# A fused attention and gated feed-forward kernel: the second query block in two halves, and the order of jobs, fetches and roots around it

## The chip, the cores and the metric

The kernel runs on one core of a Trainium2 chip. The metric is the device time of one execution in microseconds, lower is better. Each kernel is judged by the median of several runs; one further execution is profiled.

## The reference

```python
def _layernorm(x, axis=-1, eps=1e-5):
    m = jnp.mean(x, axis=axis, keepdims=True)
    v = jnp.var(x, axis=axis, keepdims=True)
    return (x - m) / jnp.sqrt(v + eps)

def reference(A_x, A_wqkv, A_wo, B_x, B_w_gate, B_w_up, B_w_down):
    def _A_ref(x, wqkv, wo):                       # B=1, S=2048, D=640, H=32, Dh=20
        qkv = (x @ wqkv).reshape(B, S, 3, H, Dh).transpose(2, 0, 3, 1, 4)
        q, k, v = qkv[0], qkv[1], qkv[2]
        scores = jnp.einsum("bhqd,bhkd->bhqk", q, k) * (Dh ** -0.5)
        p = softmax(scores)
        o = jnp.einsum("bhqk,bhkd->bhqd", p, v)
        return o.transpose(0, 2, 1, 3).reshape(B, S, D) @ wo
    def _B_ref(x, w_gate, w_up, w_down):           # F=1728
        g = x @ w_gate
        u = x @ w_up
        return (g * u) @ w_down
    h = A_x + _A_ref(_layernorm(A_x), A_wqkv, A_wo)
    return h + _B_ref(_layernorm(h), B_w_gate, B_w_up, B_w_down)
```

All tensors are bf16.

## The kernel before

**Work and tiles.** The 2048 queries are four blocks of 512 (`QB`), the 32 heads eight groups of four (`HPG`), the 2048 keys sixteen tiles of 128. A head takes a slot of 32 partitions, so the four heads of a group are computed side by side in the TensorE array. Scores are made transposed, keys on partitions. A score tile (`sc`, L533) is 1536 columns, three PSUM banks; a bank is one head and key tile against 512 queries, or two key tiles against 256 queries. ScalarE takes the exponential of a score tile into an `E` tile (L547); 683 tiles hold all scores. There are two score tiles (`slot`) and six `E` buffers. TensorE then multiplies `E` with the values (`emit_AV`, L740; a value round is up to `AV_ROUNDS` units for each head), with a column of ones that gives the softmax sums, and VectorE drains the accumulator `acc` into `asb` (L752).

**Segments.** The tiles run through a list of segments `segs`, each a pass and a group of heads. A pass is a block or half of one: "0" to "3" are whole blocks, "C" and "D" are the halves of block 2, "A" and "B" those of block 3. `SPLIT_G` groups of a split block run whole and first; then the others run for the first half and after that for the second. Blocks 0 and 1 run whole; the first four groups of block 0 run by chunks of keys, as these are projected.

**Takes.** Where `x_takes` allows it, VectorE computes the exponential of the last bank of a tile, in four instructions (L580, L590, L591, L585) into `xe`; the ScalarE instruction is then 1024 columns instead of 1536. I call this a take. Among the conditions: the segment is not one of the chunked ones, the tile holds one segment alone, at least `X_LEAST` tiles of the segment follow, fewer than `X_OUT` taken banks wait for use, VectorE isn't behind, ScalarE isn't waiting for scores, and in the last block `room()`: 700 ns (`TILE_NS`) for each tile left must exceed the outstanding jobs (`PE_NS`, and `PART_NS` for each part still to open) by more than `ROOM`.

**The order.** The program is written out tile by tile by a planner that keeps model clocks (`at`): scores of tile i, value rounds, then jobs until shortly before the next scores must go (`run_job`). Jobs are Python generators in queues (`jobs`, `urgent`, `waiting`): first the projections of keys, values and queries, then the tails. If nothing is left to run, two padding matmuls keep TensorE busy (`keep_warm`, L496). `later(n, f)` runs f n tiles on. VectorE's spare time goes to takes under way and to small generators (`aux`). The order on each engine is fixed when the program is built.

**Norms and tails.** The softmax sums of a segment are inverted and spread by transfers over SP's queue (`norm`: L636, L637, L649, L652); for the segments in `FAST` by TensorE instead (`job_norm`). When all groups of a part are normed, `add_tail` opens its tail: output projection (`job_out`, L978), layer norm with the root on GpSimd (`rstd_steps`), transposes (L283), the gated layer (`job_glu`; whole blocks L1065, halves L1083), and the down projection (`job_y`, L1129). The up and gate weights are fetched for each of seven steps (L1036, buffers for two steps); in block 3 some are resident. The queries are written to DRAM (`spill`) for a general path that runs only if the softmax sums leave their range. Transfers are issued by SP in order.

**The end.** After the last tile, `last_tail` computes the tail of B with six PSUM banks: out projection (L1230, L1234), layer norm, and, while VectorE and ScalarE normalize, `fill` runs the jobs that are left; of A's down projection the last of four half rows is `held` back for this. Then transposes, gated layer (L1065) and down projection (L1129).

Of the kernel before, what the change touches and what calls it, by code (L numbers as in the profile page):

```python
# [19 lines left out]
P = 128  # L20
# [22 lines left out]
SPLIT_G = 2  # L43
# [17 lines left out]
RES_STEPS = 3  # L61
# [24 lines left out]
def kernel(  # L86
# [42 lines left out]
    huge = const.tile([P, 1], F32, name="huge")  # L129
    wo = [const.tile([P, D], BF16, name=f"wo{g}") for g in range(NG)]  # L130
# [52 lines left out]
    nc.gpsimd.memset(huge[:], 3.0e38)  # L183
    for c in range(KT):
        nc.vector.memset(wpad[c][:].rearrange("p m h e -> p (m h) e")[:, :, DH:SLOT], 0.0)
# [18 lines left out]
    def rstd_steps(mv, n, made, ve_=None):  # L204
# [11 lines left out]
        yield 1000 if ve_ is nc.vector else 50  # L216
        y = small.tile([P, n], F32, name="y")
        ve_.tensor_scalar(y[:].bitcast(I32), v[:].bitcast(I32), -0.5, float(0x5F3759DF), ALU.mult, ALU.add)
        t = small.tile([P, n], F32, name="nt")
        for k in range(3):  # L220
            ve_.tensor_tensor(t[:], y[:], y[:], ALU.mult)
            if ve_ is nc.gpsimd:
                ve_.tensor_tensor(t[:], t[:], v[:], ALU.mult)
                ve_.tensor_scalar(t[:], t[:], -0.5, 1.5, ALU.mult, ALU.add)
                ve_.tensor_tensor(y[:], t[:], y[:], ALU.mult)
            else:
                ve_.scalar_tensor_tensor(t[:], t[:], -0.5, v[:], ALU.mult, ALU.mult)
                ve_.scalar_tensor_tensor(y[:], t[:], 1.5, y[:], ALU.add, ALU.mult)
            if k != 2:
                yield (800, 600)[k] if ve_ is nc.vector else 50  # L230
        den = small.tile([P, n], BF16, name="den")
        ve_.tensor_tensor(den[:], v[:], y[:], ALU.mult)
# [81 lines left out]
    def job_V(t, half):  # L314
        ps = bank()
        for c in range(KT):
# [12 lines left out]
            "C": (2, 0, HW), "D": (2, HW, HW), "A": (3, 0, HW), "B": (3, HW, HW)}  # L329
# [621 lines left out]
    def load_wd():  # L951
        for f in range(2 * FP):
            p0 = max(0, (f + 1) * P - FF)
            if p0:
                nc.gpsimd.memset(late["Wd"][f][0:p0, :], 0.0)
# [488 lines left out]
```

## Time and profile before

| | us |
|---|---|
| median of 3 runs | 916.38 (915.68 to 917.12) |
| the profiled execution | 916.05 |
| its span, first to last instruction | 914.0 |
| ScalarE busy | 866.2 (95%) |
| TensorE matmuls busy | 817.5 (89%) |
| VectorE busy | 702.1 (77%) |
| GpSimd busy | 57.4 (6%) |

A row of grouped instructions reads: line, engine, operation, output<-input, shapes, count | busy us, mean ns of one | idle us of the engine just before them, and what ended it. A row of the timeline: start us, length us, engine, line, operation, count, and in brackets the idle time before it with what ended it. A row of the chain of waits: start, length, what. A row of windows: the stretch, its length, then busy us and count of each engine asked for, the clock granted to TensorE as a share of full speed, the busy share of the DMA engines, GB/s. Times run from the start of the span. The mean of a ScalarE instruction includes the part in which it overlaps with the next.

### The profile page before, as it was taken

The page shows a single profiled execution, that of the slowest core. Times are in us where ns is not written, and L with a number is a line of the kernel's source. Part 1 is how long each engine was busy: PE and PEld are TensorE (multiplying, and loading weights), DVE is VectorE, ACT ScalarE, POOL GpSimd, SP SyncE. Part 2 cuts the span into 40 slices and gives each one's busy share as a digit, 9 for nine tenths or more (in the row PEclk, how much of TensorE's full clock was granted, in tenths as well). Part 3 has the DMA queues.
Part 4 walks back from the last instruction along what each step waited for, and adds up shares of the span by engine and source line. Part 5 has one row for each costly group of instructions (what it writes and reads, how often), then busy time and mean ns, then how long its engine had stood idle before and what let it go on. Part 6 is the DMA issues. An engine that isn't in the chain of part 4 may idle for free.

```text
span 914.0 us, 20094 instructions
## 1 busy us (share of the span) xinstructions
PE 817.5 (89%) x8035; PEld 346.8 (38%) x8115; DVE 702.1 (77%) x1310; ACT 866.2 (95%) x719; POOL 57.4 (6%) x255
## 2 busy tenths in 40 slices
PE   8788999889989899899897888999998999998897
PEld 5233333222223222233232333434434445444575
DVE  8664349899999899899998999798998784542243
ACT  6999999999999999999999999999999999999931
POOL 4210000000001200000003000020001000010000
PEclk9999999999999999999999999999999999999999
DMA  6000011011025022212410022021411211201310
GB/s 195 17 14 1 1 27 27 14 24 37 4 61 149 13 71 72 64 49 90 160 28 14 20 70 68 19 54 49 117 51 42 73 28 51 57 15 50 80 44 18
DMA packets 74203, 46.54 MB, mean 51 GB/s; under 512 B 20380, under 2 KB 70440, under 8 KB 74104
## 3 DMA queue, kind: packets, MB, share of 16 engines
q1 hardware_dynamic: 74104, 45.20, 18.0%
q8 instruction: 65, 1.06, 0.5%
q14 instruction: 34, 0.28, 0.1%
HBM read 37.88 MB, written 7.30 MB: 49 GB/s over the span
## 4 chain that ended last, share of the span: by engine, by line
ACT 67%; issue 17%; PE 10%; DVE 4%; DMA 1%; POOL 1%; SPq 0%; ACTq 0%
ACT E L547 67%; PE sc L533 2%; PE f L1065 2%; PE f L1129 2%; PE acc L740 1%; DVE st L201 1%; PE mi L303 1%; PE mi L978 0%; PE f L1230 0%; PE mi L496 0%; DMA wu<-in_B_w_up_dram 0%; PE mi L317 0%; PE mi L1083 0%; DVE kT L310 0%; DVE vx L270 0%
## 5 line engine op out<-in xcount | busy, mean ns | idle before, releaser
L547 ACT ACTIVATE E<-sc 128x1536 bf16<-128x1536 f32 (+1 forms) x683 | 848.7, 1417 | 6.2 <-PE sc L533 5.9
L533 PE MATMUL sc<-qa,kT 32*128 32x512 bf16 (+1 forms) x1920 | 203.2, 340 | 28.6 <-ACT E L547 16.9
L533 PEld LDWEIGHTS <-kT 32*128 32x128 bf16 x2816 | 84.1, 91 | 244.6 <-issue 206.1
L740 PE MATMUL acc<-E,vx 128*32 128x256 bf16 (+1 forms) x2592 | 170.3, 326 | 1.7 <-DVE vx L270 1.2
L580 DVE TENSOR_SCALAR xv<-sc 128x512 f32<-128x512 f32 x167 | 115.0, 689 | 30.2 <-PE sc L533 26.5
L585 DVE SCALAR_TENSOR_TENSOR xe<-xt,xv 128x512 int16<-128x512 f32 x167 | 113.3, 682 | 1.0
L591 DVE SCALAR_TENSOR_TENSOR xt<-xt,xv 128x512 f32<-128x512 f32 x167 | 112.3, 681 | 0.5
L590 DVE SCALAR_TENSOR_TENSOR xt<-xv 128x512 f32<-128x512 uint16 x167 | 112.0, 683 | 0.3
L303 PE MATMUL mi<-lnT,wp 128*128 128x512 bf16 x279 | 83.3, 381 | 11.7 <-DVE qa L310 5.5
L740 PEld LDWEIGHTS <-vx 128*32 128x32 bf16 x2816 | 55.8, 95 | 66.4 <-issue 63.8
L533 PE MATMUL sc<-qb,kT 32*128 32x256 bf16 (+1 forms) x896 | 68.2, 288 | 8.1 <-ACT E L547 5.3
L1129 PE MATMUL mi<-wd,hh 128*128 128x320 bf16 x336 | 58.2, 301 | 1.6 <-DVE xr L1133 1.6
L740 PE MATMUL acc<-xe,vx 128*32 128x512 bf16 (+1 forms) x224 | 50.6, 332 | 0.0
L1129 PEld LDWEIGHTS <-hh 128*128 128x128 bf16 x448 | 38.7, 97 | 30.6 <-issue 18.7
L303 PEld LDWEIGHTS <-wp 128*128 128x128 bf16 x310 | 25.0, 97 | 55.9 <-issue 44.3
L310 DVE TENSOR_SCALAR kT<-mi,one_row 128x512 bf16<-128x512 f32 x30 | 22.5, 750 | 28.1 <-PE mi L303 24.7
L1065 PE MATMUL mi<-ln2T,wg 128*128 128x512 bf16 x128 | 38.0, 382 | 5.8 <-DVE u L270 5.2
L496 PE MATMUL mi<-kT,ident 128*128 128x512 bf16 x116 | 37.8, 386 | 5.5 <-DVE ln2T L270 1.0
L978 PE MATMUL mi<-wo,on 128*128 128x320 bf16 x224 | 40.5, 301 | 2.2 <-DVE xr L982 2.0
L1065 PE MATMUL mi<-ln2T,wu 128*128 128x512 bf16 x128 | 37.3, 382 | 4.3 <-DVE hh L1073 3.5
L1083 PE MATMUL mi<-ln2T,qa 128*128 128x256 bf16 x240 | 34.6, 274 | 4.1 <-DVE hh L1091 3.0
L207 POOL CAST mb<-mv 128x2 bf16<-128x2 f32 (+1 forms) x10 | 2.3, 231 | 528.6 <-DVE mv L202 410.9
(143 smaller groups left out, 645.0 us busy)
## 6 DMA issues: line engine op xcount, KB each, us to landing
wu<-in_B_w_up_dram SPq DMA_DIRECT2D x23, 320.0 KB
wg<-in_B_w_gate_dram SPq DMA_DIRECT2D x23, 320.0 KB
bc<-scr SPq DMA_DIRECT2D x80, 64.0 KB
qsp<-qa SPq DMA_DIRECT2D x8, 384.0 KB
xr<-in_A_x_dram SPq DMA_DIRECT2D x16, 160.0 KB
bc<-scr SPq DMA_DIRECT2D x76, 32.0 KB
out_dram<-xr SPq DMA_DIRECT2D x14, 160.0 KB
wd<-in_B_w_down_dram SPq DMA_DIRECT2D x13, 160.0 KB
```

What stands on the lines that cost most here:

```text
L303: nc.tensor.matmul(ps[:], lhsT=wslice(m, g, c), rhs=lnT[:, c, ch * QB:(ch + 1) * QB], start=(c == 0), stop=(c == KT - 1))
L496: nc.tensor.matmul(ps[:], lhsT=ident[:], rhs=kT[0][:, 0:BANK], start=True, stop=True)
L533: nc.tensor.matmul(sc[:, o:o + w], lhsT=kT[g][SLOT * j:SLOT * (j + 1), kt * P:(kt + 1) * P], rhs=q_of(g, b, c0, w)[SLOT * j:SLOT * (j + 1) ...
L547: exps = nc.scalar.activation(e[:, 0:n_act], sc[:, 0:n_act], ACT.Exp, bias=EXP_BIAS, scale=SM_SCALE)
L580: took = nc.vector.tensor_scalar(v[:], ps, X_SCALE, X_BASE, ALU.mult, ALU.max)
L585: nc.vector.scalar_tensor_tensor(e[:], t[:], X_R, v[:], ALU.mult, ALU.add)
L590: lambda: nc.vector.scalar_tensor_tensor(t[:], u, X_P, u, ALU.add, ALU.mult),
L591: lambda: nc.vector.scalar_tensor_tensor(t[:], t[:], X_Q, u, ALU.add, ALU.mult),
L740: nc.tensor.matmul(acc["t"][SLOT * j:SLOT * (j + 1), 0:w], lhsT=vx[kt][:, VS * h:VS * h + SLOT], rhs=e, start=(acc["n"][j] == 0), stop=(ac ...
L978: nc.tensor.matmul(ps[:, 0:HALF], lhsT=on[g][:, t * P:(t + 1) * P], rhs=wo[g][:, cs], start=(g == 0), stop=(g == NG - 1))
L1065: nc.tensor.matmul(ps[:, 0:n], lhsT=st["w", fp][k][:, c, f_cols(fp, f2)], rhs=st["ln2T"][:, c, c0:c0 + n], start=(c == 0), stop=(c == KT - 1))
L1129: nc.tensor.matmul(ps[:, 0:HALF], lhsT=st["hh"][f // 2][:, f % 2, t * P:(t + 1) * P], rhs=late["Wd"][f][:, cs], start=(f == 0), stop=(f == ...
```

## The change

- Block 1 gets four whole groups and then four groups in halves, the passes "E" and "F"; block 3 has one whole group instead of two. Each half of block 1 has a tail of its own; the tables of what a tail waits for follow.
- `job_ahead`: before the value rounds of a tile, a job that is under way runs on, as long as the round still fits before the next scores.
- The weights of block 0's tail, the down weights and the spill are issued tile by tile through `later` instead of in one go.
- `load_up`: in the gated layer of a half, the up weight of the step after the next is fetched when the up half of a step is done; its gate weight comes with the usual call.
- In `rstd_steps`, which runs on GpSimd, the square root is one `pow` by 0.5 instead of a first guess and three rounds of four instructions.
- At the end, if `fill` has run for less than `LN_NS` in the model, padding matmuls make up the rest.
- `X_OUT` 6 to 5, `ROOM` 5000 to 2500; `asb` gets three buffers instead of two.

```diff
-SPLIT_G = 2
+SPLIT_G = {"1": 4, "2": 2, "3": 1}
...
+LN_NS = 3300
...
-X_LEAST, X_OUT, X_SOON = 2, 6, 4
+X_LEAST, X_OUT, X_SOON = 2, 5, 4
...
-PART_NS, TILE_NS, ROOM = 31500, 700, 5000
+PART_NS, TILE_NS, ROOM = 31500, 700, 2500
...
         v = small.tile([P, n], F32, name="v")
         ve_.tensor_copy(v[:], ve[:])
-        yield 1000 if ve_ is nc.vector else 50
-        y = small.tile([P, n], F32, name="y")
-        ve_.tensor_scalar(y[:].bitcast(I32), v[:].bitcast(I32), -0.5, float(0x5F3759DF), ALU.mult, ALU.add)
-        t = small.tile([P, n], F32, name="nt")
-        for k in range(3):
...
         den = small.tile([P, n], BF16, name="den")
-        ve_.tensor_tensor(den[:], v[:], y[:], ALU.mult)
+        ve_.tensor_tensor(den[:], v[:], half[:, 0:n], ALU.pow)
...
-    segs += [("1", g, 0, NT, "only") for g in range(NG)]
-    for full, halves in ("2", "CD"), ("3", "AB"):
-        segs += [(full, g, 0, NT, "only") for g in range(SPLIT_G)]
-        segs += [(p, g, 0, NT, "only") for p in halves for g in range(SPLIT_G, NG)]
+    for full, halves in ("1", "EF"), ("2", "CD"), ("3", "AB"):
+        segs += [(full, g, 0, NT, "only") for g in range(SPLIT_G[full])]
+        segs += [(p, g, 0, NT, "only") for p in halves for g in range(SPLIT_G[full], NG)]
     FINAL = len(segs) - 1
-    TAILS = {0: [0], 1: [0], 2: [0, 2]}
-    FAST = {("C", NG - 1), ("D", NG - 1), ("A", NG - 1), ("B", NG - 2)}
+    TAILS = {0: [0], 1: [0, 2], 2: [0, 2]}
+    FAST = {("E", NG - 1), ("F", NG - 1), ("C", NG - 1), ("D", NG - 1), ("A", NG - 1), ("B", NG - 2)}
...
-            if c == FREE and cur["key"][0] not in ("spill", "load"):
+            if c == FREE and cur["key"][0] != "load":
...
+    def av_ns(upto):
...
+        if sum(rows) < min(most * HPG, left) and min(u[0] for u in av_q) > upto - E_BUFS + 3:
+            return 0
+        return SWITCH + -(-sum(rows) // HPG) * (w * 5 // 12 + 4)
+
+    def job_ahead(upto):
+        ns = av_ns(upto)
+        if not ns:
+            return
+        until = max(at["exp"] - S_EXP - MARGIN, at["slot"][-2]) - ns
+        if not cur["fresh"]:
+            run_job(until)
...
-                asb = parts[g] if kind == "copy" else nrm.tile([P, QB], F32, name="asb")
+                asb = parts[g] if kind == "copy" else nrm.tile([P, QB], F32, name="asb", bufs=3)
...
-    COLUMNS_OF = {(1, 0): (0, 0), (1, 2): (0, 0), (2, 0): (1, 0), (2, 2): (1, 0), (3, 0): (2, 0)}
+    COLUMNS_OF = {(1, 0): (0, 0), (1, 2): (0, 0), (2, 0): (1, 0), (2, 2): (1, 2), (3, 0): (2, 0)}
...
+    def load_up(fp, st):
+        if ("w", fp) not in st and fp not in late["next"] and fp not in st["res"]:
+            st["up", fp] = [w_tile(B_w_up, fp, late["w"].tile([P, KT * FPW], BF16, name="wu"))]
...
-    def glu_two(st, fp, c0, n):
+    def glu_two(st, fp, c0, n, up_done):
...
+            if k == 0:
+                up_done()
             yield NEXT
...
-                yield from glu_two(st, fp, c0, n)
+                far = order[k + 2] if order[1] not in st["res"] and k + 2 < FP else None
+                yield from glu_two(st, fp, c0, n, lambda: far is not None and load_up(far, st))
...
-    HELD_BY = {(1, 0): [(0, 0)], (2, 0): [(0, 2)], (2, 2): [(1, 0)], (3, 0): [(1, 2)]}
+    HELD_BY = {(1, 0): [], (1, 2): [(0, 0)], (2, 0): [(0, 2)], (2, 2): [(1, 0)], (3, 0): [(1, 2)]}
...
-                load_w(0, tail_st[b])
-                load_w(1, tail_st[b])
-                load_wd()
+                for fp in range(2):
+                    later(4 * fp + 3, lambda fp=fp: load_w(fp, tail_st[b]))
+                for f in range(2 * FP):
+                    later(WD_AT + WD_STEPS * f, lambda f=f: load_wd(f))
...
-                do(("spill", g), lambda g=g: spill(g))
+                later(SPILL_AT + 4 * g, lambda g=g: spill(g))
...
+        begun = at["pe"]
         fill()
+        warm_ps = bank()
+        for _ in range(int((LN_NS - (at["pe"] - begun)) / 216)):
+            nc.tensor.matmul(warm_ps[:], lhsT=ident[:], rhs=kT[0][:, 0:BANK], start=True, stop=True)
...
-    due = [("0", range(NG), 0, [0, 1, 2, 3]), ("1", range(NG), 1, [0, 1, 2, 3]), ("C", range(SPLIT_G, NG), 2, [0, 1]),
-           ("D", range(SPLIT_G, NG), 2, [2, 3]), ("A", range(SPLIT_G, NG), 3, [0, 1])]
+    due = [("0", range(NG), 0, [0, 1, 2, 3]), ("E", range(SPLIT_G["1"], NG), 1, [0, 1]), ("F", range(SPLIT_G["1"], NG), 1, [2, 3]), ("C", range(SPLIT_G["2"], NG), 2, [0, 1]),
+           ("D", range(SPLIT_G["2"], NG), 2, [2, 3]), ("A", range(SPLIT_G["3"], NG), 3, [0, 1])]
...
+        if LAG <= i < n_tiles:
+            job_ahead(i - 2)
         for _ in range(2):
             emit_AV(i if i >= n_tiles else i - 2 if i >= LAG else i - 3)
```

More of the change, by code (lines that the diff above doesn't have):

```diff
@@ L129 @@
     huge = const.tile([P, 1], F32, name="huge")
+    half = const.tile([P, TPB], F32, name="half")
     wo = [const.tile([P, D], BF16, name=f"wo{g}") for g in range(NG)]
@@ L705 @@
     final = {}
+    def av_ns(upto):
+        if not av_q or acc["seg"] not in (None, av_q[0][1]):
+            return 0
+        s = av_q[0][1]
+        if acc["seg"] is None and at["pe"] < at["acc"] and now["i"] < acc["from"] and min(u[0] for u in av_q) > now["i"] - E_BUFS:
+            return 0
+        w = PASS[segs[s][0]][2]
+        most, rows = AV_ROUNDS * QB // w, [0] * HPG
+        for u in av_q:
+            if u[0] > upto or u[1] != s:
+                break
+            rows[u[3]] = min(rows[u[3]] + 1, most)
+        left = acc["left"] if acc["seg"] == s else END_OF_TIME
+        if sum(rows) < min(most * HPG, left) and min(u[0] for u in av_q) > upto - E_BUFS + 3:
+            return 0
+        return SWITCH + -(-sum(rows) // HPG) * (w * 5 // 12 + 4)
[6 more added lines that the diff above has]
+            run_job(until)
     def emit_AV(upto):
@@ L934, in spill @@
     def spill(g):
+        if ("spill", g) in done:
+            return
+        done.add(("spill", g))
         nc.sync.dma_start(qsp[g][:, 0:QA], qa[g][:])
@@ L1161, in rows_early @@
         key = b, ts[0]
-        if key in HELD_BY and key not in rows_in and all(("y",) + k in done for k in HELD_BY[key]):
+        if key in HELD_BY and key not in rows_in and ("open",) in done and all(("y",) + k in done for k in HELD_BY[key]):
             rows(b, ts)
```

37 lines of the change are left out of this document (14 added, 23 removed).

## The prediction

> **What bounds the kernel now.** I read the page's table of busy times first, then ScalarE's groups by shape, then ScalarE's timeline, then the chain of work at the end.
>
> ```profile
> PE 817.5 (89%) x8035; PEld 346.8 (38%) x8115; DVE 702.1 (77%) x1310; ACT 866.2 (95%) x719; POOL 57.4 (6%) x255
> L547 ACT ACTIVATE E<-sc 128x1536 bf16<-128x1536 f32 x515 | 717.2, 1520 | 5.7 <-PE sc L533 5.5
> L547 ACT ACTIVATE E<-sc 128x1024 bf16<-128x1024 f32 x168 | 178.2, 1100 | 0.5 <-PE sc L533 0.5
> 59.03 430.35 ACT L547 ACTIVATE E<-sc 128x1536 bf16<-128x1536 f32 x350 [0.29 <-PE sc L533]
> 489.60 19.53 ACT L547 ACTIVATE E<-sc 128x1536 bf16<-128x1536 f32 x16 [0.22 <-PE sc L533]
> 509.62 250.99 ACT L547 ACTIVATE E<-sc 128x1024 bf16<-128x1024 f32 x206 [0.49 <-PE sc L533]
> 761.44 108.46 ACT L547 ACTIVATE E<-sc 128x1536 bf16<-128x1536 f32 x82 [0.84 <-PE sc L533]
> ```
>
> ScalarE runs exponentials (L547) almost without a break until 761.44 + 108.46 = 869.9 us. In that whole stage it idles 5.7 + 0.5 = 6.2 us: 0.22 + 0.49 + 0.84 = 1.55 us of it after 59 us, the other 4.65 us in the start. So there are four ways to save time: fewer columns for ScalarE, fewer of these gaps, a shorter start, a shorter end. The first way is priced by the two shapes: where VectorE takes one bank of 512 columns from a tile (a "take"), ScalarE's instruction is 1520 − 1100 = 420 ns shorter. There were 168 short ones, one of which is the rest at the end, so 167 takes.
>
> The end, after 869.9 us, belongs to TensorE, as the chain of waits and the timeline show:
>
> ```profile
> 876.15 7.67 PE f L1129 x56
> 883.82 0.28 PE mi L283 x5
> 885.15 11.08 PE f L1065 x100
> 900.80 7.70 PE f L1129 x56
> 878.28 1.12 DVE L1257 TENSOR_SCALAR ln<-f,m,rstd 128x320 bf16<-128x320 f32 x2
> 878.44 1.13 ACT L1258 ACTIVATE ln<-f,mr,rstd 128x320 bf16<-128x320 f32 x2 [0.48 <-DVE mr L1253]
> ```
>
> The last rows' normalized values are ready at 878.28 + 1.12 = 879.40 and 878.44 + 1.13 = 879.57 us. But their transposes (L283) start at 883.82, because 56 matmuls of the part before (A's down projection, put there by `fill`) still hold TensorE. Some cover is needed there, but it is 883.82 − 879.57 = 4.25 us too long.
>
> **The change, part by part.**
>
> *The second block in halves.* Where does TensorE lack work it could do earlier?
>
> ```profile
> L496 PE MATMUL mi<-kT,ident 128*128 128x512 bf16 x46 | 14.3, 385 | 0.0
> 431.24 0.39 PE L496 MATMUL mi<-kT,ident 128*128 128x512 bf16 x1
> 432.10 0.60 PE L496 MATMUL mi<-kT,ident 128*128 128x512 bf16 x2
> 463.74 0.72 PE L978 MATMUL mi<-wo,on 128*128 128x320 bf16 x4
> ```
>
> From 431.24 to 463.74 us, 32.5 us, the job queue is empty: block 0's tail is done, block 1's is not open, and TensorE runs padding (L496; 46 of them between 425 and 475 us). A second padding matmul behind a first adds 0.60 − 0.39 = 0.21 us, so 46 are about 9.7 us of matmul time. With E done half a block before F, E's tail is there for this hole. All later jobs then stand up to 9.7 us of matmul time further ahead, more than the 7.67 us of A's down projection that are now left for the end. That is the first reason to expect A to be finished in time.
>
> The second is SPLIT_G 2 → 1 for the last block. A, and B behind it, have seven groups instead of six and the whole groups are one fewer: A ends one half group, 64·256 / 1536 = 10.7 tiles, earlier. At 108.46 / 82 = 1.32 us a tile that is 14.1 us more before the end.
>
> Do halves cost TensorE time? Score tiles and value rounds of both widths stand in the timeline:
>
> ```profile
> 489.10 0.39 PE L533 MATMUL sc<-qa,kT 32*128 32x512 bf16 x3
> 844.79 0.40 PE L533 MATMUL sc<-qb,kT 32*128 32x256 bf16 x6 [0.20 <-ACT E L547]
> 484.81 0.62 PE L740 MATMUL acc<-E,vx 128*32 128x512 bf16 x8
> 845.12 0.62 PE L740 MATMUL acc<-E,vx 128*32 128x256 bf16 x16
> ```
>
> Six narrow ones take 0.40 us and three wide ones 0.39; sixteen and eight both take 0.62. So I cost the narrow form at 0 on TensorE. On VectorE each of the five groups newly split adds a drain, a reciprocal and a product; bounded by 0.69 us each (rows of the takes, below) that is at most 5 × 3 × 0.69 = 10.4 us, four takes, and at least nothing; narrow drains are shorter, and I use one take.
>
> *The takes.* What VectorE does in the last 120 us is the largest unknown. One take is four instructions, and the windows show how many fit:
>
> ```profile
> L580 DVE TENSOR_SCALAR xv<-sc 128x512 f32<-128x512 f32 x167 | 115.0, 689 | 30.2 <-PE sc L533 26.5
> L585 DVE SCALAR_TENSOR_TENSOR xe<-xt,xv 128x512 int16<-128x512 f32 x167 | 113.3, 682 | 1.0
> L591 DVE SCALAR_TENSOR_TENSOR xt<-xt,xv 128x512 f32<-128x512 f32 x167 | 112.3, 681 | 0.5
> L590 DVE SCALAR_TENSOR_TENSOR xt<-xv 128x512 f32<-128x512 uint16 x167 | 112.0, 683 | 0.3
> 300.00:425.00 125.00, 22.76 (x33) 1.00 0.22 56
> 525.00:650.00 125.00, 21.44 (x31) 1.00 0.20 52
> 750.00:870.00 120.00, 3.96 (x6) 1.00 0.18 48
> 300.00:425.00 125.00, 113.84 (x877) 38.21 (x889) 113.18 (x192) 125.00 (x104) 3.99 (x15) 1.00 0.22 56
> 750.00:870.00 120.00, 108.53 (x1487) 59.59 (x1488) 50.22 (x101) 119.14 (x92) 3.60 (x19) 1.00 0.18 48
> ```
>
> A take costs 0.689 + 0.682 + 0.681 + 0.683 = 2.735 us of VectorE. The first three window rows are those of L580 alone: 33 takes begin in 125 us of whole groups, 31 in 125 us of halves, 6 in the last 120 us. In the last two rows VectorE (third figure) is 113.18 / 125 = 91% busy in the middle and 50.22 of 120 us at the end. There `room()` refuses takes: it asks whether the jobs outstanding fit into the tiles left. With jobs earlier, and ROOM 5000 → 2500 (2500 / 700 = 3.6 tiles longer), it says yes for longer. If the last 120 us filled to 91%, there would be (0.91 × 120 − 50.2) / 2.735 = 21 more takes; if `room()` stayed shut, none. I take 10, since A's GLU, charged whole with 19,500 ns until it ends, must still shut it for a stretch. Against it: one take for the extra drains; and 33 → 31 takes per 125 us for half segments, over 5 × 21.3 = 107 tiles, some 140 us, two takes. What E's tail displaces in the hole comes back later, where it no longer has to be done. X_OUT 6 → 5 can only refuse takes; I put 0 on it, with a bound of the few that stand open at a time. So +7 takes, 7 × 0.42 = 2.9 us off; bounds from 3 lost to 21 won, +1.3 to −8.8 us.
>
> *The end.* With A's down projection out, all but the last of its four half rows (`held`), `fill` gives 14 matmuls, 7.67 × 14/56 = 1.9 us, and the new padding stretches this to LN_NS, 3.3 us. The normalized values arrive at 879.57, 3.4 us after 876.15; so the transposes start about 879.9 instead of 883.82: −3.9 us. If A is not done, nothing changes: 0.
>
> *Fetches.* One gap of ScalarE comes from a weight:
>
> ```profile
> 756.23 0.42 SPq L1036 DMA_DIRECT2D wu<-in_B_w_up_dram  x1
> 759.73 1.27 PE L1083 MATMUL mi<-ln2T,wu 128*128 128x256 bf16 x10 [1.03 <-DMA wu<-in_B_w_up_dram]
> ```
>
> The up weight was issued at 756.23 and TensorE stood 1.03 us for it; the scores queued behind it on TensorE came late, hence the 0.84 us at 761.44. `load_up` issues the up weight of step k+2 as soon as step k's up half is done, half a step sooner. That should close this gap. The 0.22 and 0.49 us at 489 and 509 us lie where block 1's tail waited for its own norms with no other job; with jobs of an earlier half there they can close too. So up to −1.55 us. But E and F need 14 pairs of weights where block 1 needed 7, all through SP's queue, where norm transfers wait too; I allow one new gap of 0.84. Net −0.7. The spread-out loads of block 0 (first weights, down weights, spill) move SP issues and no engine's work; its cover is block 0's projections, which TensorE still runs then: 0, and if a load comes too late, one gap of 0.84.
>
> *Jobs ahead of values.* In the start a gap looks like this:
>
> ```profile
> 36.37 0.62 PE L740 MATMUL acc<-E,vx 128*32 128x512 bf16 x8
> 38.80 0.39 PE L533 MATMUL sc<-qa,kT 32*128 32x512 bf16 x3 [0.85 <-DVE kT L310]
> ```
>
> A value round of 0.62 us stood between scores and a key projection; the projection's drain was late, and the next scores waited 0.85 us for it. `job_ahead` puts the open job in front of such a round, so its drain comes up to 0.62 us sooner. Only tiles from LAG (10) on qualify, and the 4.65 us of start gaps are not all of this form. Waiting on TensorE behind the moved matmuls is the value round, and behind it the freeing of E buffers, of which there are six. Bounds: −4.65 if all gaps close, +0.62 for one round that comes too late; I take −0.6.
>
> *GpSimd's root.*
>
> ```profile
> L223 POOL TENSOR_TENSOR nt<-nt,v 128x2 f32<-128x2 f32 (+1 forms) x30 | 8.0, 265 | 2.4
> DVE rstd L238 <- POOL den L232: 2.0, 2, 1.1
> 26.60 0.20 POOL L232 TENSOR_TENSOR den<-v,y 128x4 bf16<-128x4 f32 x1
> 28.13 0.17 DVE L238 RECIPROCAL rstd<-den 128x4 f32<-128x4 bf16 x1
> ```
>
> Thirteen small instructions per root go (one first guess, three rounds of four), at 265 ns some 3.4 us of latency; GpSimd is 6% busy. No row shows a power. Cheap, like a product, it ends VectorE's two waits (2.0 us in all, beside a busy ScalarE: 0 for the end). It may cost 3.4 us more than a product before a root is later than now, and the reciprocal has slack (26.80 to 28.13) as well. I take 0; bounds −0.2 and, for one late root in the start, +1.1 (below).
>
> The sum: −2.9 − 3.9 − 0.7 − 0.6 = −8.1 us. The profiled execution took 916.05 us (span 914.0 and 2.05 around it), 0.33 under the median 916.38, less than 0.2% (1.8 us), which is about what a measurement here can tell from no change. So 916.05 − 8.1 = 908.0 us.
>
> **The rivals.**
>
> *Full gain in takes.* `room()` stays open nearly throughout: 21 takes instead of 7 net, 14 × 0.42 = 5.9 us more, 902.1 us. For it: the 58% of VectorE that idles at the end. Against: TensorE at 108.53 of 120 us there, and takes are only begun where scores are on time. Chance 0.15.
>
> *The halves come too late for the end.* E's tail fills the hole, but the queue stays as long as before, since every part has waits of its own; A's down projection stays at the end and `room()` stays shut. Then only −0.7 − 0.6 and perhaps half of the end, −2, remain: 912.8 us. Chance 0.17.
>
> *The first power is late.* The first root is ready at 26.80 us, its reciprocal begins at 28.13: slack of 1.33 us, and the 3.4 us saved come on top. Each microsecond by which a power is longer than a product beyond these 4.7 holds VectorE at L238, then the key drain queued behind it, then scores and ScalarE. Late by as much again as the slack, it gives 908.0 + 1.3 = 909.3 us. Against: the other small operations of GpSimd take 0.2 to 0.3 us. Chance 0.05. [...]
>
> *Slower: weights through one queue.* Place: the GLU steps of E and F, 14 pairs of fetches. SP issues in order; a fetch stands behind norm transfers that wait for VectorE, TensorE stands for the weight, and scores behind it are late. Price: the 0.84 us of 761.44 each time. With all 14, 11.8 us, and what the change gains otherwise, 8.1: 919.8 us. It decides from 8.1 / 0.84 = 10 such stalls. For it: the halves' steps are half as long and fetch as much. Against: C and D fetch the same 14 pairs today with one stall, and the change issues sooner. Chance 0.17, with smaller mishaps of TensorE's order under this sign.
>
> **How the numbers follow.** Forecast 0.41, takes 0.15, too late 0.17, first power 0.05, slower 0.17; the 0.05 left are for gains and losses that cancel within 0.2%. Faster by over 0.2%: 0.41 + 0.15 + 0.17 + 0.05 = 0.78; within: 0.05; slower: 0.17. The low end takes all bounds together only nearly: 908.0 − 5.9 (takes) − 2.0 (half of the start gaps) = 900. The high end takes in the too-late case with one lost take per split and one stall more: 912.8 + 2.1 + 0.84 = 915.7, and no change beside it: 916.5. Outside stay the slower case and a rest.
>
> **What would show it.** Right: no run of L496 of over 30 us near 430 us; out projections (L978) there instead; at least seven more short exponentials; takes going on after 800 us; transposes 3.4 to 4 us after the last out matmuls, with six or so padding matmuls before them; fewer than 14 instructions in GpSimd's roots. Wrong: 56 matmuls of L1129 still between the out projection and the transposes; TensorE waits for wu or wg in E and F with ScalarE gaps behind; fewer than 167 takes; a power of over 3.4 us.

## The result, and the profile after

The changed kernel takes 911.82 us (median of 7 runs, 910.36 to 913.58) against 916.42 (7 runs, 915.61 to 917.76): a ratio of 0.9949, 95% interval 0.9939 to 0.9958. It is 4.6 us faster, a little over half of the 8.1 us that the prediction's sum came to. The profiled execution took 910.57 us, with a span of 908.7; it is one of the two shortest of the seven.

The page's busy times, ScalarE's two shapes, and ScalarE's timeline from 59 us on; then the page's row for all exponentials, of the kernel before and of the changed one:

```profile
PE 828.4 (91%) x8894; PEld 371.0 (41%) x8894; DVE 736.3 (81%) x1381; ACT 862.0 (95%) x719; POOL 32.9 (4%) x126
L534 ACT ACTIVATE E<-sc 128x1536 bf16<-128x1536 f32 x502 | 700.1, 1505 | 7.1 <-PE sc L520 3.8 <-PE acc L752 2.5
L534 ACT ACTIVATE E<-sc 128x1024 bf16<-128x1024 f32 x181 | 189.3, 1078 | 0.0
58.89 263.85 ACT L534 ACTIVATE E<-sc 128x1536 bf16<-128x1536 f32 x211 [0.29 <-PE sc L520]
323.12 155.08 ACT L534 ACTIVATE E<-sc 128x1536 bf16<-128x1536 f32 x128 [0.38 <-PE acc L752]
478.70 52.56 ACT L534 ACTIVATE E<-sc 128x1536 bf16<-128x1536 f32 x43 [0.50 <-PE acc L752]
531.88 25.33 ACT L534 ACTIVATE E<-sc 128x1536 bf16<-128x1536 f32 x21 [0.63 <-PE acc L752]
557.69 169.75 ACT L534 ACTIVATE E<-sc 128x1536 bf16<-128x1536 f32 x139 [0.47 <-PE acc L752]
727.99 138.84 ACT L534 ACTIVATE E<-sc 128x1536 bf16<-128x1536 f32 x112 [0.55 <-PE acc L752]
```

```profile
L547 ACT ACTIVATE E<-sc 128x1536 bf16<-128x1536 f32 (+1 forms) x683 | 848.7, 1417 | 6.2 <-PE sc L533 5.9
L534 ACT ACTIVATE E<-sc 128x1536 bf16<-128x1536 f32 (+1 forms) x683 | 844.4, 1392 | 7.1 <-PE sc L520 3.8
```

There are 181 short exponentials instead of 168, so 13 more takes, 13 × 0.42 = 5.5 us. But the last exponential ends at 727.99 + 138.84 = 866.83 instead of 869.92, only 3.1 us sooner. Three things make up the difference. The first exponential starts at 16.0 instead of 15.6 us (in all the traces it lies between 15.5 and 16.2). All exponentials together are busy for 844.4 instead of 848.7 us, which is 4.3 us less and not 5.5; why a take brings less than 0.42 us here, no run shows. And ScalarE idles 0.9 us more between them, 7.1 for 6.2: behind scores it waits less, 3.8 for 5.9 us, but the brackets show five gaps "<-PE acc L752", 2.5 us in all, that the kernel before did not have. There ScalarE waits for a value round, because the E tile it is to write isn't free yet.

VectorE's first instruction of a take (L567) in the windows, the padding between 425 and 475 us, the chain at the end, and the transposes in the timeline:

```profile
300.00:425.00 125.00, 23.46 (x34) 1.00 0.29 85
525.00:650.00 125.00, 21.76 (x32) 1.00 0.28 74
750.00:870.00 120.00, 14.77 (x22) 1.00 0.14 35
L483 PE MATMUL mi<-kT,ident 128*128 128x512 bf16 x4 | 1.2, 384 | 0.0
867.27 1.60 PE mi L1151 x11
874.56 3.80 PE f L1151 x28
879.71 11.08 PE f L1084 x100
878.20 0.44 PE L271 MATMUL mi<-ident,ln 128*128 128x128 bf16 x5
```

The hole is filled: 4 padding matmuls instead of 46. The takes come where the prediction looked for them, 22 instead of 6 in the last 120 us; the rest of the kernel has 3 fewer. The gated layer starts 879.71 − 866.83 = 12.9 us after the last exponential, before 885.15 − 869.92 = 15.2: 2.3 us shorter. A's down projection is not done, though: 11 matmuls still stand in front of the out projection (1.6 us) and 28, not 14, between it and the transposes. So no padding of LN_NS is issued.

### The profile page after: what moved, and what is told of

Read it like the earlier page. It is cut to its first block, busy times and chain, and to the rows that moved or that the text cites. A ratio compares the mean times of both kernels' runs of the same rounds, so it can differ in the third digit from the quotient of the medians.

```text
span 908.7 us, 21741 instructions
## 1 busy us (share of the span) xinstructions
PE 828.4 (91%) x8894; PEld 371.0 (41%) x8894; DVE 736.3 (81%) x1381; ACT 862.0 (95%) x719; POOL 32.9 (4%) x126
## 4 chain that ended last, share of the span: by engine, by line
ACT 55%; PE 21%; issue 15%; DVE 8%; DMA 1%; SPq 0%; DVEq 0%; ACTq 0%
ACT E L534 55%; PE sc L520 5%; PE mi L1102 4%; PE acc L752 3%; PE mi L1151 2%; PE f L1084 2%; PE f L1151 1%; DVE st L204 1%; DVE xv L567 1%; DVE u L1107 1%; PE mi L483 1%; DVE xt L578 1%; PE mi L1084 1%; PE mi L992 1%; DVE xe L572 0%
## 5 line engine op out<-in xcount | busy, mean ns | idle before, releaser
L534 ACT ACTIVATE E<-sc 128x1536 bf16<-128x1536 f32 (+1 forms) x683 | 844.4, 1392 | 7.1 <-PE sc L520 3.8
L520 PE MATMUL sc<-qa,kT 32*128 32x256 bf16 (+1 forms) x2176 | 203.7, 318 | 19.6 <-ACT E L534 11.7
L752 PE MATMUL acc<-E,vx 128*32 128x256 bf16 (+1 forms) x2849 | 169.2, 310 | 1.8 <-DVE vx L258 1.2
L567 DVE TENSOR_SCALAR xv<-sc 128x512 f32<-128x512 f32 x180 | 124.1, 690 | 38.0 <-PE sc L520 35.1
L578 DVE SCALAR_TENSOR_TENSOR xt<-xt,xv 128x512 f32<-128x512 f32 x180 | 121.4, 682 | 0.6
L577 DVE SCALAR_TENSOR_TENSOR xt<-xv 128x512 f32<-128x512 uint16 x180 | 120.5, 682 | 0.2
L752 PEld LDWEIGHTS <-vx 128*32 128x32 bf16 x3136 | 65.7, 96 | 68.7 <-issue 65.0
L752 PE MATMUL acc<-xe,vx 128*32 128x256 bf16 (+1 forms) x287 | 56.0, 303 | 0.0
L1102 PE MATMUL mi<-ln2T,wg 128*128 128x256 bf16 x270 | 38.7, 274 | 4.9 <-DVE u L1107 4.5
L1102 PE MATMUL mi<-ln2T,wu 128*128 128x256 bf16 x270 | 39.3, 274 | 1.7 <-DVE hh L1110 1.6
L1107 DVE CAST u<-mi 128x512 bf16<-128x512 f32 x35 | 24.0, 686 | 11.9 <-PE mi L1102 11.6
L305 PE MATMUL mi<-wv,lnT 128*128 128x320 bf16 x160 | 28.5, 300 | 5.0 <-DVE vx L258 3.0
```

What stands on the lines that cost most here:

```text
L520: nc.tensor.matmul(sc[:, o:o + w], lhsT=kT[g][SLOT * j:SLOT * (j + 1), kt * P:(kt + 1) * P], rhs=q_of(g, b, c0, w)[SLOT * j:SLOT * (j + 1) ...
L534: exps = nc.scalar.activation(e[:, 0:n_act], sc[:, 0:n_act], ACT.Exp, bias=EXP_BIAS, scale=SM_SCALE)
L567: took = nc.vector.tensor_scalar(v[:], ps, X_SCALE, X_BASE, ALU.mult, ALU.max)
L577: lambda: nc.vector.scalar_tensor_tensor(t[:], u, X_P, u, ALU.add, ALU.mult),
L578: lambda: nc.vector.scalar_tensor_tensor(t[:], t[:], X_Q, u, ALU.add, ALU.mult),
L752: nc.tensor.matmul(acc["t"][SLOT * j:SLOT * (j + 1), 0:w], lhsT=vx[kt][:, VS * h:VS * h + SLOT], rhs=e, start=(acc["n"][j] == 0), stop=(ac ...
```

## The experiments

Each is the changed kernel with one or two parts undone or altered, but for e5. Takes are counted in the instructions; the clock is the median over the runs of the mean clock granted to TensorE. What a part is worth is given below as a difference of medians. The runs were made in three groups, and the kernel before, run with each, had medians of 916.96 (e1 to e4), 916.47 (e5 to e8) and 916.60 us (the others), so half a microsecond of such a difference says nothing. `X_OUT`, `ROOM` and the third `asb` buffer have no run of their own.

| | takes | median us | ratio to before, interval | clock |
|---|---|---|---|---|
| changed kernel | 180 | 911.82 | 0.9949 (0.9939–0.9958) | 0.995 |
| e1, no job_ahead | 176 | 914.49 | 0.9975 (0.9963–0.9987) | 0.994 |
| e2, job_ahead only with a free buffer | 181 | 912.43 | 0.9954 (0.9936–0.9972) | 0.994 |
| e3, block 1 whole | 173 | 914.03 | 0.9971 (0.9959–0.9983) | 0.998 |
| e4, e2 and ROOT_NS 1500 | 182 | 910.50 | 0.9932 (0.9916–0.9948) | 0.9965 |
| e5, kernel before with halves only | 169 | 917.70 | 1.0013 (1.0000–1.0026) | 0.9935 |
| e6, block 3 with two whole groups | 174 | 911.34 | 0.9946 (0.9933–0.9960) | 0.9985 |
| e7, long roots, their own order | 179 | 917.80 | 1.0006 (0.9994–1.0019) | 0.9915 |
| e8, no load_up | 180 | 920.76 | 1.0040 (1.0023–1.0058) | 0.989 |
| e9, long roots, same order | 180 | 919.17 | 1.0023 (1.0008–1.0037) | 0.9895 |
| e10, neither job_ahead nor load_up | 176 | 916.82 | 1.0010 (0.9992–1.0028) | 0.9935 |
| e11, ROOT_NS 3000 | 180 | 911.90 | 0.9943 (0.9929–0.9958) | 0.9945 |
| e12, fetches at once | 177 | 918.62 | 1.0024 (1.0009–1.0038) | 0.990 |

### e1 and e2: where the new gaps come from

```diff
-        if LAG <= i < n_tiles:
-            job_ahead(i - 2)
```

> The changed kernel without the call of job_ahead, all else as changed. The order as written out holds 176 takes instead of 180 (counted in the instructions): 4 x 0.427 us = 1.7 us more for ScalarE. Theory: the five gaps of ScalarE behind value rounds (2.5 us, new in the changed kernel) come from jobs put in front of a round whose E buffer the next exponential waits for. Then they vanish here, and the time is that of the changed kernel + 1.7 - 2.5, about 911 us (ratio to before 0.994). Rival: they come from the denser order (halves, more takes) and stay; then about 913.5 us (0.997).

```diff
-        if not ns:
+        if not ns or min(u[0] for u in av_q) <= upto - E_BUFS + 2:
             return
```

> The changed kernel, where job_ahead does nothing if the oldest value unit not yet used is of tile i-6, that is, if the exponential just emitted waits for its buffer. The order holds 181 takes (one more, -0.4 us). Theory: the five gaps behind value rounds go, 2.5 us, so 0.4 + 2.5 = 2.9 us less than the changed kernel, about 909 us (0.9918). Rival: the round would be late without the job too, the gaps stay: about 911.4 us (0.9945).

ScalarE's shapes in e1, then in e2:

```profile
L534 ACT ACTIVATE E<-sc 128x1536 bf16<-128x1536 f32 x506 | 704.7, 1503 | 10.3 <-PE sc L520 9.2 <-ACT E L534 0.3 <-PE acc L752 0.2
L534 ACT ACTIVATE E<-sc 128x1024 bf16<-128x1024 f32 x177 | 185.2, 1076 | 1.7 <-PE acc L752 0.8 <-PE sc L520 0.6
```

```profile
L534 ACT ACTIVATE E<-sc 128x1536 bf16<-128x1536 f32 x501 | 698.6, 1504 | 6.8 <-PE sc L520 3.9 <-PE acc L752 2.1
```

Then the changed kernel before the gap at 531.88:

```profile
529.09 0.41 DVE L764 COPY asb<-acc 128x256 f32<-128x256 f32 x1
531.39 0.62 PE L752 MATMUL acc<-E,vx 128*32 128x256 bf16 x16
```

Without job_ahead the gaps behind value rounds shrink from 2.5 to 0.2 + 0.8 = 1.0 us, but the time rises by 2.7 us where 4 takes explain 1.7: the theory's 911 us is missed, and the time comes near the rival's, though the gaps did not stay as the rival had it. (The profiled run of e1 is its slowest, 918.76 us; its waits for scores, 9.2 + 0.6 us, may be more than those of the others.) In e2 the gaps stay (2.1 us), the rival's case, and the time is the changed kernel's. Over all traces these gaps come to 1.6 to 3.7 us with job_ahead and to 0 to 1.6 us without it (the kernel before, e1, e5, e10). So job_ahead brings most of the changed kernel's, but not by holding up a round whose buffer is due at that moment.

In the traces such a gap follows the short last round of a segment. VectorE has to drain the accumulator before the next segment's first round, and the units pile up meanwhile. In three of the five places that round starts within 0.4 us of the drain's end. In the other two it comes 1.1 and 1.9 us later, as in the rows above, where the drain ends at 529.50 and the round begins at 531.39, and matmuls of a job stand in front of it. No run changed either by itself, so what the gaps come from in the end stays open.

### e3, e5 and e6: what the halves are worth

e3 takes SPLIT_G for block 1 to 8 and puts the old tables back; e6 is one figure; e5 puts the halves, with their tables, into the kernel before.

```diff
-SPLIT_G = {"1": 4, "2": 2, "3": 1}
+SPLIT_G = {"1": 8, "2": 2, "3": 1}        # e3, with the tables of before
+SPLIT_G = {"1": 4, "2": 2, "3": 2}        # e6
```

> The changed kernel with block 1 whole, its tail opened in one piece, all else as changed. The order holds 173 takes (7 fewer: +3.0 us). Theory: the halves of block 1 are what lets takes go on in the last block, by filling the hole at 430 us with the first half's tail: the hole of padding is back, about 914.8 us (0.998). Rival: halves are paid for elsewhere (14 more pairs of weights, more drains), and whole is as fast as the changed kernel: 911.8 us (0.995).

> The kernel before with block 1 in halves E and F and the tables that go with it (and, for room in memory, three asb buffers and X_OUT 5, which on the kernel before change no take), nothing else of the change. The order holds 169 takes instead of 167 and leaves less of the jobs for the end: in the planner's clocks the stretch from the last exponential to the normalized rows' cover is 6.9 us instead of 10.1. Theory (the halves fill the hole at 430 us, but the takes that this frees need the last block's earlier A and the smaller ROOM): 2 x 0.427 = 0.9 us and up to 3.2 us at the end, ratio to before 0.9955 to 0.998. Rival 1 (halves bring the whole gain by themselves): 0.9945 or less. Rival 2 (the 14 extra pairs of weights and the drains cost what the hole gives): 0.999 to 1.001.

> The changed kernel with two whole groups in block 3 (SPLIT_G 3: 2), as before the change. A ends 10.7 tiles later. The order holds 174 takes, six fewer than the changed kernel: +2.6 us; the cover at the end is longer by 1.5 us in the planner's clocks. Theory (A's earlier start is what opens the last block to takes): ratio to before 0.9975 to 0.999, takes falling off after about 800 us. Rival (block 1's halves do it, the last split only shifts): as the changed kernel, 0.9945 to 0.995.

Padding of 425 to 475 us in e3 and in e5, then the takes of 750 to 870 us in e3, e5 and e6:

```profile
L483 PE MATMUL mi<-kT,ident 128*128 128x512 bf16 x66 | 20.0, 384 | 0.0
```

```profile
L495 PE MATMUL mi<-kT,ident 128*128 128x512 bf16 x2 | 0.8, 383 | 0.5 <-DVE ln2T L270 0.5
```

```profile
750.00:870.00 120.00, 6.16 (x9) 1.00 0.18 46
```

```profile
750.00:870.00 120.00, 5.53 (x8) 1.00 0.17 43
```

```profile
750.00:870.00 120.00, 11.03 (x16) 1.00 0.12 32
```

With block 1 whole, the hole is back, the last 120 us have 9 takes, and 2.2 us are lost: the theory's order of size, somewhat less than its 3.0. Halves alone fill the hole too, but give 8 takes there, and no time: rival 2. So filling the hole opens takes only together with the rest; which part of the rest, `ROOM` above all, no run tried. In e6 six takes are lost as counted, and no time: the rival's time, though not by the rival's way. The runs of e3 and e6 had a higher clock than the changed kernel's, 0.998 and 0.9985 against 0.995 (below), so what their takes are worth is not shown clean.

### e7 and e9: the root

e7 puts the first guess and the three rounds back as they were; e9 without the `yield`s, so that TensorE, VectorE and ScalarE hold the changed kernel's instructions in its order.

```diff
-        ve_.tensor_tensor(den[:], v[:], half[:, 0:n], ALU.pow)
+        y = small.tile([P, n], F32, name="y")
+        ve_.tensor_scalar(y[:].bitcast(I32), v[:].bitcast(I32), -0.5, float(0x5F3759DF), ALU.mult, ALU.add)
+        ...
+        ve_.tensor_tensor(den[:], v[:], y[:], ALU.mult)
```

> The changed kernel with the first guess and three rounds in place of the power. The order holds 179 takes (one fewer, +0.4 us). Theory: since the order still keeps 5000 ns between root and use, the power gives latency that nothing takes up: 0 to 0.5 us, ratio 0.9945 to 0.9955. Rival: the 13 small instructions per root cost VectorE time (waits at the root, slower instructions beside GpSimd): 1.5 us or more, 0.9965.

> The changed kernel with the first guess and three rounds in place of the power, but issued in one piece as the power is, so that TensorE, VectorE, ScalarE and SP hold the same instructions in the same order as in the changed kernel (180 takes); only GpSimd's roots are longer. e7_long_roots had another order as well. [...] Rival: e7 lost by its other order of jobs, the latency is covered by the 5000 ns kept for it: 0.9945 to 0.9955.

The two powers' rows in the changed kernel, then e9's timeline where the two roots of block 0's tail are made one after the other:

```profile
L220 POOL TENSOR_TENSOR den<-v,half 128x2 bf16<-128x2 f32 x7 | 6.3, 900 | 0.6
L220 POOL TENSOR_TENSOR den<-v,half 128x4 bf16<-128x4 f32 x3 | 3.1, 1041 | 0.3
```

```profile
306.60 0.17 DVE L238 RECIPROCAL rstd<-den 128x2 f32<-128x2 bf16 x1 [3.26 <-POOL den L232]
307.85 0.47 DVE L270 COPY ln2T<-mi 128x640 bf16<-128x640 bf16 x1
308.38 1.01 PE L495 MATMUL mi<-kT,ident 128*128 128x512 bf16 x2 [3.46 <-DVE ln2T L270]
310.04 1.02 ACT L546 ACTIVATE E<-sc 128x1024 bf16<-128x1024 f32 x1 [3.51 <-PE sc L532]
```

A power takes 0.9 to 1.04 us in the mean and replaces fourteen instructions. In e9 it is missing, with the order unchanged, and 7.4 us are lost against the changed kernel: the longer root costs this time, and the other order of e7, which e9's rival blames, does not. Slower instructions beside GpSimd, which e7's rival names, do not show in the kernel before, whose roots are the long ones: there L580 takes 685 ns in the mean where GpSimd is busy for more than half of its time (11 of 167) and 689 ns elsewhere. One way of the loss can be read down the rows. GpSimd works through two roots in series, the last steps of which begin at 301.00 and 306.37 us; VectorE stands 3.26 us at the reciprocal; the drain of a transpose queued behind it is late; TensorE stands 3.46 us at its next instruction, which happens to be padding that wants the same bank; ScalarE gets no scores for 3.51 us.

This is not all of it. ScalarE's waits for scores are 12.0 us in e9 and 3.8 us in the changed kernel. Of the 8.2 us more, 4.0 lie at this root (3.51, and 0.50 right behind it). Of the rest, 2.2 us lie at 668 to 675 us and 1.9 us at 871 to 873 us, where VectorE waits for no root. That the long root brings these on too is not shown. The mean clock of e9's profiled run is 0.988, that of the changed kernel's 0.999.

### e8 and e10: the up weights

```diff
-                far = order[k + 2] if order[1] not in st["res"] and k + 2 < FP else None
+                far = None
```

> The changed kernel without load_up: the up weight of a half's GLU step is fetched when the step before begins, as before the change. The order is the same for every other instruction, 180 takes. Theory: waits of TensorE for up weights come back (none in the changed kernel, one of 1.03 us before), each with a gap of ScalarE of 0.84 us; E, F, C and D have 28 steps: one to four gaps, +0.8 to 3.4 us, ratio 0.9955 to 0.998. Rival: the fetches were in time anyway, ratio 0.9945 to 0.995 and no wait on a weight in the trace.

> The changed kernel without job_ahead and without load_up. Order as e1_no_ahead but for the up weights, 176 takes. Theory: the up weights come late only because job_ahead packs the GLU steps closer (e5_halves_only, without either, waited 0.2 us for weights in all): near e1_no_ahead, 0.9975 to 0.999. Rival: the halves' steps need the earlier fetch whatever the order of jobs and rounds: five waits and more as in e8_no_load_up, 1.005 or above.

Waits and timeline of e8, then the waits of e10:

```profile
PE mi L1102 <- DMA wu<-in_B_w_up_dram: 5.7, 5, 2.0
719.08 0.72 PE L1102 MATMUL mi<-ln2T,wu 128*128 128x256 bf16 x5 [1.88 <-DMA wu<-in_B_w_up_dram]
720.25 1.02 ACT L534 ACTIVATE E<-sc 128x1024 bf16<-128x1024 f32 x1 [1.74 <-PE sc L520]
```

```profile
PE mi L1102 <- DMA wu<-in_B_w_up_dram: 1.7, 1, 1.7
```

Without load_up TensorE waits five times for up weights, up to 2.0 us, and 8.9 us are lost. The theory named the mechanism but undersized it. The trace shows less than the median: it is of the shortest run, 917.13 us at a clock of 0.995, and what the others lose beyond that goes with a lower clock, and no trace of them is there to show it. Without job_ahead as well, one wait is left, and only 5.0 us are lost; 1.0010 lies between theory and rival. So job_ahead makes the early fetch urgent, but not alone. In the changed kernel there is no such wait.

### e12: the fetches in one go

```diff
-                for fp in range(2):
-                    later(4 * fp + 3, lambda fp=fp: load_w(fp, tail_st[b]))
-                for f in range(2 * FP):
-                    later(WD_AT + WD_STEPS * f, lambda f=f: load_wd(f))
+                load_w(0, tail_st[b])
+                load_w(1, tail_st[b])
+                for f in range(2 * FP):
+                    load_wd(f)
...
-                later(SPILL_AT + 4 * g, lambda g=g: spill(g))
+                do(("spill", g), lambda g=g: spill(g))
```

> The changed kernel with the first weights, the down weights and the spill of block 0's tail issued as before the change, in one go and as jobs. The order holds 177 takes, three fewer: +1.3 us. Theory: norm transfers and the first GLU weights queue behind the burst on SP, and jobs come late: 2 us or more beside the takes, 0.998 or above. Rival: block 0's tail has cover enough, only the takes differ: 0.9955 to 0.9965.

Its timeline up to 283 us:

```profile
264.54 8.99 SPq L970 DMA_DIRECT2D wd<-in_B_w_down_dram  x14
274.73 0.51 SPq L623 DMA_DIRECT2D sums<-asb  x1
279.46 0.25 DVE L634 RECIPROCAL ri<-sums_all 128x16 f32<-128x16 f32 x1 [4.36 <-DMA sums_all<-sums]
280.71 2.29 PE L992 MATMUL mi<-wo,on 128*128 128x320 bf16 x8 [3.75 <-DVE xr L996]
283.64 2.37 ACT L534 ACTIVATE E<-sc 128x1024 bf16<-128x1024 f32 x2 [4.79 <-PE sc L520]
```

The theory's norm transfer is there: the softmax sums of a segment are issued behind the burst, VectorE stands 4.36 us for them, an out projection's drain is late behind that, and ScalarE loses 4.79 us in one gap. A late first weight does not show. This run is the shortest of twelve, 914.70 us at a clock of 0.998; the median is 3.9 us longer at 0.990, and no trace shows where. The three loads were put back together, so which of them matters is open; the rows point to the down weights (`wd`).

### e4 and e11: a shorter wait for the root

```diff
-WO_NS, SUMS_NS, ROOT_NS, ROWS_NS = 1500, 6000, 5000, 5000
+WO_NS, SUMS_NS, ROOT_NS, ROWS_NS = 1500, 6000, 3000, 5000   # e11; e4: 1500, and the line of e2
```

> As e2_ahead_free, and the wait that the order keeps between GpSimd's root and VectorE's use of it, ROOT_NS, is 1500 ns instead of 5000: the order had kept the time of the long root, though the short one is done in 2.3 us. It holds 182 takes, and A's down projection is done, but for the held half row, when the last exponential ends; in the changed kernel 11 of its matmuls (1.6 us) and two half rows (28 matmuls, 3.8 us) were left. Theory: -0.85 us for two takes, -1.6 us, and 2.5 us of gaps: about 906.9 us (0.9896). Rival: VectorE now stands for roots that are not ready (2.3 us against 1.5, ten times, behind it drains), and the gain is lost: 910 us or more (0.993).

> The changed kernel with ROOT_NS 3000 instead of 5000. The order holds 180 takes, and A's down projection is done, but for the held half row, before the last exponential ends, so that 11 matmuls (1.6 us) and a half row (1.9 us) leave the end and padding makes up the cover of 3.3 us. In e4_root1500 (1500 ns) VectorE stood 3.2 us for roots, and its end was 1.6 us shorter than the changed kernel's. Theory: with 3000 ns hardly a wait at the roots, end shorter by 1.6 to 2 us: 909.5 to 910.5 us, 0.9920 to 0.9930. Rival: the root is needed at 5000 ns anyway, and the gain at the end is lost as waits or as half-clock windows: 0.9945.

The chain at the end of e11:

```profile
874.91 1.90 PE f L1151 x14
876.82 1.29 PE f L1286 x6
878.11 0.45 PE mi L271 x5
879.62 11.08 PE f L1084 x100
```

Here the end is what the prediction drew: 14 matmuls, six of padding (L1286), then the transposes. The last exponential ends at 868.57, so the gated layer starts 11.05 us after it, 15.2 − 11.05 = 4.2 us sooner than in the kernel before. The time is nevertheless the changed kernel's (0.9943), as the rival had it: the last exponential ends 1.7 us later, with ScalarE's waits for scores at 6.1 us against 3.8. In e4 VectorE stands for roots, as its rival had it (3.2 us, four times), the gaps behind value rounds are 3.7 us instead of gone, and it is still the lowest median, 910.50. Its interval, 0.9916 to 0.9948, overlaps the changed kernel's; that it beats it is not shown. It beats the kernel before.

## Why the prediction was right, and where it wasn't

**What bounds the kernel, and the way of the gain:** right. E's tail fills the hole, takes go on after 800 us, the end is shorter, and the up weight's wait is gone. **Narrow matmuls at no cost:** nearly. In the changed kernel the windows from 525 to 650 us hold 32 takes beside them, and all scores and value rounds together keep TensorE busy for 272.1 and 174.8 us, 0.7 and 1.5 us more than before.

The forecast lies 3.8 us below the measured median. In the two profiled executions the spans differ by 5.3 us, and the rows give this in the terms of the sum:

| term | forecast | rows | what they show |
|---|---|---|---|
| takes | −2.9 | −4.3 | busy time of all exponentials |
| end | −3.9 | −2.2 | from the last exponential to the last instruction |
| fetches | −0.7 | −1.5 | the three gaps after 59 us are gone |
| jobs ahead, in the start | −0.6 | −0.5 | from the first exponential to 59 us |
| gaps behind value rounds | at most +0.6 | +2.5 | the five brackets |
| nothing in the sum | 0 | +0.8 | first exponential 0.4 us later, smaller gaps 0.4 us more |

They add up to 5.2 us. That the medians differ by 4.6 is for the most part because the profiled execution of the changed kernel is 1.25 us below its median, that of the kernel before 0.4.

**The takes** were undersized, 13 for 7: 16 more came in the last 120 us where the prediction took 10 between none and 21, and 3 fewer elsewhere, as forecast. At its price of 0.42 us they would be 5.5 us; the rows give 4.3. **The end** was oversized. The failed step is that an A that ends 10.7 tiles earlier and the hole's 9.7 us suffice to finish A's down projection. They don't with the 5000 ns that the order keeps for a root; e11 shows it done with 3000. **Fetches:** load_up left no wait for a weight, and no new gap came.

**Jobs ahead.** The gain in the start came out as forecast. The gap at 54.60 us of the kernel before is gone in the changed kernel, whose exponentials run on from 47.52, and it is back without job_ahead, in e1:

```profile
54.60 4.13 ACT L547 ACTIVATE E<-sc 128x1536 bf16<-128x1536 f32 x3 [0.54 <-PE sc L533]
47.52 11.08 ACT L534 ACTIVATE E<-sc 128x1536 bf16<-128x1536 f32 x8 [1.13 <-PE sc L520]
54.43 4.13 ACT L534 ACTIVATE E<-sc 128x1536 bf16<-128x1536 f32 x3 [0.54 <-PE sc L520]
```

(Of the 4.65 us that the prediction puts in the start, the timeline shows 4.4; the rest is small gaps all over.) The failed step is the price of job_ahead: the prediction named the freeing of E buffers as what stands behind the moved matmuls, and then bounded it at one round of 0.62 us. It is five gaps, 2.5 us, of which 1.0 are left without it. That the kernel without it is slower all the same (e1) is for the most part the four takes that its order holds less.

That the time came out well inside the range is in part luck: takes and fetches brought more than forecast, the end and the new gaps less.

**GpSimd's root** at 0 and **the spread-out loads** at 0 failed as prices of these edits in the new order: undone, they cost 7.4 and 6.8 us, and load_up 8.9 instead of the 0.84 allowed. Each had been costed in the order of the kernel before, where the two waits at roots (0.9 and 1.1 us) stand beside no gap of ScalarE of over 0.22 us, and the sums came in time. No run puts one of them alone into that kernel, so there the zeros may hold. In the denser order the slack is gone. The same holds for the halves: alone they are worth nothing (e5), taken from the rest 2.2 us (e3). The parts undone cost 2.7 + 2.2 + 8.9 + 7.4 + 6.8 = 28 us, the change as a whole brings 4.6, and load_up and job_ahead undone together cost less than load_up alone. They are not terms of a sum, and the prediction treated them as such.

**The rival "too late"** came true in part: A's down projection stayed, for the most part, at the end. **"Slower: weights through one queue"** is what e8 shows, with five waits; load_up is what prevents it, so its evidence against held. **"The first power is late"** did not happen: the first power, at 23.4 us, is one of 1.04 us, and the reciprocal keeps its place at 28.5.

**A term was missing** altogether: the clock, below. In the main comparison it can't be much, as the kernel before has medians of 0.996 to 0.997 and the changed kernel 0.995; in the experiments it goes down to 0.989.

## What to carry to other kernels

Where engines issue in order, price an edit in the order it will run in: a latency that is covered today (a root, a sum's transfer, a weight) can be a stall of three engines once the order around it is packed closer (at e9's root 3.26, 3.46 and 3.51 us). A part that is worth nothing alone may be what keeps the others' gain, so undo parts from the whole as well as adding them to the old kernel. And when the bound engine is fed by another, look at whether that one's clock fell where it waited (in e9 from 0.99 to 0.50 at 306.10 us).

## What the runs showed of the hardware

The clock granted to TensorE falls to half in these traces, as for a stretch of 3.42 us in the kernel before and for two of 3.40 us, one behind the other, in e9, also where TensorE was not idle just before. Three stretches of the kernel before (PE, PEld, DVE, ACT, POOL, then the clock):

```profile
486.40:489.81 3.41, 1.80 (x20) 0.81 (x15) 2.88 (x7) 3.19 (x4) 0.00 (x0) 1.00 0.09 27
501.87:505.28 3.41, 2.04 (x36) 0.79 (x35) 2.88 (x7) 3.41 (x4) 2.09 (x9) 1.00 0.02 5
505.28:508.70 3.42, 3.09 (x29) 0.99 (x30) 3.10 (x6) 3.42 (x3) 0.00 (x0) 0.50 0.04 6
```

In the second TensorE shows 2.04 us busy of 3.41, and the one after it is granted half. In the first it shows less, 1.80 us, and the clock stays full until 505.28. In e9 the clock falls at 306.10 us, in the middle of the stall, and stays at half for two stretches:

```profile
302.70:306.10 3.40, 1.95 (x20) 0.69 (x20) 0.64 (x2) 3.40 (x4) 2.41 (x13) 0.99 0.24 56
306.10:309.50 3.40, 1.12 (x5) 0.21 (x4) 2.65 (x6) 0.42 (x1) 0.98 (x3) 0.50 0.51 144
309.50:312.90 3.40, 3.40 (x22) 0.90 (x19) 2.06 (x4) 2.37 (x2) 0.00 (x0) 0.50 0.02 5
```

So the stretches just before the falls were 60% and 57% busy by the profile, and not idle.

The busy share alone does not tell when it happens, though. In e1, too, a stretch as thin as the one at 501.87, 2.06 us of 3.41, is followed by the full clock, and one that is 81% busy is followed by half:

```profile
664.00:667.41 3.41, 2.06 (x25) 0.88 (x21) 2.94 (x7) 3.41 (x4) 0.00 (x0) 1.00 1.10 275
667.41:670.83 3.42, 3.13 (x29) 1.44 (x29) 3.38 (x6) 3.42 (x4) 0.00 (x0) 1.00 1.14 317
776.60:780.00 3.40, 2.75 (x41) 1.43 (x36) 3.33 (x7) 3.40 (x4) 0.00 (x0) 1.00 0.24 77
780.03:783.40 3.37, 3.37 (x31) 1.10 (x31) 2.27 (x8) 2.75 (x3) 0.00 (x0) 0.50 0.00 0
```

What goes with it in time shows between runs of one kernel. In e1 the run with a mean clock of 0.997 took 913.21 us and that with 0.987 took 918.76: 5.55 us for 0.010 of clock, that is 0.010 × 917 × 2 = 18 us at half clock, if full and half, the two that the stretches show, are all there is. By that slope, 0.0055 of clock between the changed kernel and e9 would be 3.1 of its 7.4 us, and 0.0035 between it and e6 would be 1.9 us the other way, about what e6's six takes (2.6 us) cost. The slope is rough: straight lines through the runs of each kernel give 440 to 790 us for a whole unit of clock, where this pair gives 555. Clock and stall need not be separate causes: a stall can thin the stretch (in e9 the 3.46 us of TensorE begin in the one that is 57% busy), and a halved clock lengthens what follows: six score matmuls of the kernel before take 0.40 us from 501.99 us on and 0.62 from 506.94, three of e9 0.39 us from 304.54 and 0.61 from 309.33. No run held the clock up by itself, so these shares are argued, not shown.
